# Eight opening transposes written as identity matmuls into fp32 PSUM, in a fused gated mix of a state-space layer and a GELU MLP

## Chip, cores, metric

One core of a Trainium2 chip. The metric is the device time of one execution in microseconds (us). The kernel before takes 213.1 us (median of the six runs that stood beside the result, 212.7 to 213.45).

## The reference, cut to what matters

```python
x = A_x                                            # 1 x 2048 x 640, bf16
g = sigmoid((x * gate_w).sum(-1, keepdims=True))
a = ssm(x, Lambda, B, C, log_dt, Dskip)            # complex diagonal recurrence over 2048 steps
b = gelu(x @ w1 + b1) @ w2 + b2                    # 640 -> 1728 -> 640
return g * a + (1 - g) * b                         # bf16
```

Only the start of `x @ w1` matters here. The kernel multiplies with the 640 features of x on partitions, so x has to be transposed first.

## The kernel before

The first 512 rows of x are wanted as soon as possible. Features 0 to 255 of them are loaded as they lie and transposed by TensorE (eight blocks of 128 x 128); the rest comes through transposing DMAs. Meanwhile TensorE is kept busy by seven matmuls on constants, whose results nobody reads. TensorE's results go into PSUM, in this program eight banks of 512 fp32 columns (`PS[0]` to `PS[7]`), and VectorE copies the transposed blocks from there into `xT`, which the matmuls read. The parts that matter (cuts marked):

```python
load("xna", "sp", ..., xn[0][:, :, 0:256], x2[0:512, 0:256]...)     # 1st transfer of the queue
w1load(0, "sp", 1)            # 2nd: w1 rows 0-127, columns 0-1023 -> tokens ("w1", 0, ...)
w1load(1, "sp", 1.3)          # ... then the other slices
WSPLIT = {1: 6, 3: 6}         # slices that come in two transfers: first 6 column blocks, then 2
...
def f_warm():                                                      # L415
    for n in (512,) * 6 + (256,):
        t = nc.tensor.matmul(PS[4][:, 0:n], one.broadcast_to([128, 128]), one.broadcast_to([128, n]), start=True, stop=True)
    return inc("pe", t)
op("warm", "pe", 2.7, (), [("bank", 4)], f_warm, prio=-1000)

for i, (k, c0, c1) in enumerate(((0, 0, 2), (0, 2, 4), (1, 0, 2), (1, 2, 4))):
    bank = (7, 6, 5, 4)[i]
    pt = PS[bank][:, :].bitcast(BF16)[:, 0:(c1 - c0) * 128]
    def f_xt(k=k, pt=pt, c0=c0, c1=c1):                            # L427: two transposes a bank
        for c in range(c0, c1):
            t = nc.tensor.transpose(pt[:, (c - c0) * 128:(c - c0 + 1) * 128], xn[0][:, c, k * 128:(k + 1) * 128], ident[:, :])
        return inc("pe", t)
    op(f"xt{i}", "pe", ..., ["xna", "ident"], [("bank", bank)], f_xt, prio=-990 + i)
    def f_xc(k=k, pt=pt, c0=c0, c1=c1):                            # L433: VectorE copy PSUM -> SBUF, bf16
        return inc("dve", nc.vector.tensor_copy(out=xT[0][:, k, c0 * 128:c1 * 128], in_=pt))
    op(f"xc{i}", "dve", 0.42, [("bank", bank)], [("xT", 0, k, c0)], f_xc, prio=-2000 + i)
...
# m1_first (L640): x @ w1 for the first 512 rows; the first four matmuls take halves of 256 columns
steps = [(0, 0, 0), (0, 1, 0), (0, 0, 1), (0, 1, 1)] + [(k, jf, None) ...]
```

L640 is the first real work of TensorE; L662 is the rest of `x @ w1`. One line lower in the changed kernel: L641 and L663; the copies are L434 there.

## Time and profile before

| | before |
|---|---|
| span in the profile | 212.1 us |
| TensorE busy | 208.0 us, 98% |
| last of the eight transposes starts | 4.42 us |
| first W1 slice lands | 5.12 us |
| first L640 matmul starts | 5.25 us |
| first L662 matmul starts | 14.34 us |

How to read it: TensorE is nearly always busy, so whatever delays it in the opening delays the end by as much; the lines that show this stand in the prediction. Two instants are worth keeping apart in the opening: when the first weights land, and when TensorE goes from half to full speed. The second can be read without any clock counter from the distance between starts: 256 columns take 213 ns at half speed and 108 at full, 512 columns 427 and 216.

### The profile page before, as it was taken

How to read it: one execution, taken by the hardware profiler on the slowest of the kernel's cores; microseconds unless marked ns; L12 is line 12 of the kernel's file. 1: busy time of each engine (PE TensorE's matmuls, PEld its weight loads, DVE VectorE, ACT ScalarE, POOL GpSimd, SP SyncE). 2: the span in 40 equal slices, each digit the busy share in tenths (PEclk: the TensorE clock that was granted, in tenths of full speed). 3: DMA queues.
4: the chain of work that ended last, by engine and by line, in shares of the span. 5: the costliest groups of instructions: out<-in, count | busy, mean ns of one | idle time of the engine just before them, and what ended most of it. 6: DMA issues, size and time to landing. Idle time of an engine off the chain costs nothing.

```text
span 212.1 us, 2737 instructions
## 1 busy us (share of the span) xinstructions
PE 208.0 (98%) x1088; PEld 104.9 (49%) x1102; DVE 190.1 (90%) x240; ACT 103.0 (49%) x177; POOL 4.2 (2%) x12
## 2 busy tenths in 40 slices
PE   7999999999999999999999999999999999999996
PEld 3444444444564444444464444444446444567775
DVE  2399999999999999999999999899999999499744
ACT  2389556677960353556681063455660027623330
POOL 1000000030000000000000000000010000000000
DMA  5999999999600010075274000004742000005251
GB/s 163 202 279 135 207 171 198 380 222 162 185 12 3 0 49 0 0 85 111 54 59 114 3 0 0 0 2 115 96 96 117 0 3 0 0 0 104 68 140 63
DMA packets 48808, 19.08 MB, mean 90 GB/s; under 512 B 41500, under 2 KB 47772, under 8 KB 48796
## 3 DMA queue, kind: packets, MB, share of 16 engines
q1 hardware_dynamic: 47136, 17.59, 39.7%
q0 software_dynamic: 1600, 1.32, 4.5%
q8 instruction: 8, 0.13, 0.4%
q14 instruction: 4, 0.03, 0.1%
q10 hardware_dynamic: 60, 0.01, 0.0%
HBM read 8.41 MB, written 2.63 MB: 52 GB/s over the span
## 4 chain that ended last, share of the span: by engine, by line
PE 96%; DMA 2%; issue 1%; SPq 0%; DVE 0%
PE ps L662 22%; PE ps L705 20%; PE ps L929 20%; PE ps L978 15%; PE ps L792 7%; PE ps L841 5%; PE ps L640 4%; DMA W1sb<-in_B_w_dram 2%; PE ps L683 1%; PE ps L940 1%; PE ps L806 0%; SPq L333 0%; DVE W1sb L875 0%; PE ps L446 0%
## 5 line engine op out<-in xcount | busy, mean ns | idle before, releaser
L662 PE MATMUL ps<-xT,W1sb 128*128 128x512 bf16 x215 | 47.5, 379 | 0.3
L745 DVE TENSOR_TENSOR_SCAN W<-atab,V 128x1280 bf16<-128x1280 f32 x16 | 44.3, 2812 | 0.3
L705 PE MATMUL ps<-xT,BT 128*128 128x512 bf16 x196 | 43.1, 379 | 0.3 <-issue 0.2
L929 PE MATMUL ps<-Gl,W2sb 128*128 128x512 bf16 (+1 forms) x230 | 42.5, 343 | 0.2
L669 ACT ACTIVATE Gl<-ps,cols 128x512 bf16<-128x512 f32 x44 | 29.9, 694 | 15.5 <-PE ps L662 15.5
L662 PEld LDWEIGHTS ps<-xT,W1sb 128*128 128x128 bf16 x220 | 21.6, 98 | 25.9
L978 PE MATMUL ps<-Hb,CT 128*128 128x512 bf16 x150 | 32.9, 379 | 0.0
L929 PEld LDWEIGHTS ps<-Gl,W2sb 128*128 128x128 bf16 x234 | 22.9, 98 | 19.3
L705 PEld LDWEIGHTS ps<-xT,BT 128*128 128x128 bf16 x200 | 19.5, 98 | 23.7 <-ACT Gt L691 0.4
L714 ACT ACTIVATE U<-ps 128x512 bf16<-128x512 f32 x40 | 23.6, 599 | 14.6 <-PE ps L705 14.5
L947 ACT ACTIVATE E1T<-ps,cols 128x512 bf16<-128x512 f32 (+1 forms) x18 | 9.5, 624 | 36.0 <-PE ps L940 36.0
L978 PEld LDWEIGHTS ps<-Hb,CT 128*128 128x128 bf16 x150 | 14.5, 98 | 17.9 <-DVE V L496 0.6
L986 ACT ACTIVATE E2T<-ps 128x512 bf16<-128x512 f32 x15 | 9.1, 604 | 13.6 <-PE ps L978 13.6
L792 PE MATMUL ps<-W2sb,Gl 128*128 128x320 bf16 x104 | 14.8, 299 | 0.0
L615 DVE SCALAR_TENSOR_TENSOR trf<-xn,gwb 128x640 bf16<-128x640 bf16 x16 | 13.2, 823 | 0.4
L496 DVE TENSOR_TENSOR V<-V,W 128x1280 bf16<-128x1280 bf16 x16 | 12.5, 822 | 0.3
L496 DVE TENSOR_TENSOR Hb<-Hb,V 128x1280 bf16<-128x1280 bf16 x16 | 12.5, 822 | 0.3
L496 DVE TENSOR_TENSOR V<-mr,U 128x2560 bf16<-128x2560 bf16 x8 | 11.9, 1492 | 0.3
L792 PEld LDWEIGHTS ps<-W2sb,Gl 128*128 128x128 bf16 x104 | 10.1, 98 | 4.3 <-issue 0.3
L496 DVE TENSOR_TENSOR Hb<-c,W 128x2560 bf16<-128x2560 bf16 x8 | 11.9, 1491 | 0.2
L496 DVE TENSOR_TENSOR W<-mi,U 128x2560 bf16<-128x2560 bf16 x8 | 11.9, 1484 | 0.0
L496 DVE TENSOR_TENSOR V<-s,W 128x2560 bf16<-128x2560 bf16 x8 | 11.9, 1484 | 0.0
(91 smaller groups left out, 150.8 us busy)
## 6 DMA issues: line engine op xcount, KB each, us to landing
W2sb<-in_B_w_dram SPq DMA_DIRECT2D x1, 2080.0 KB, 8.9
out_dram<-xn SPq DMA_DIRECT2D x3, 640.0 KB, 4.8
xn<-in_A_x_dram POOLq DMA_DIRECT2D x2, 640.0 KB, 7.3
W1sb<-in_B_w_dram SPq DMA_DIRECT2D x3, 256.0 KB, 3.7
trf<-grow SPq DMA_DIRECT2D x3, 256.0 KB, 5.3
xn<-in_A_x_dram SPq DMA_DIRECT2D x1, 640.0 KB, 7.7
W1sb<-in_B_w_dram SPq DMA_DIRECT2D x1, 480.0 KB, 4.6
out_dram<-W1sb SPq DMA_DIRECT2D x3, 160.0 KB, 1.8
```

The costliest lines, as they stand in the source:

```text
L496: return inc("dve", nc.vector.tensor_tensor(out=o, in0=a, in1=b, op=o_))
L615: t = inc("dve", nc.vector.scalar_tensor_tensor(out=scr[:, :], in0=xn[q % 2][:, c, :], scalar=1.0, in1=gwb[:, :], op0=ALU.mult, op1=ALU.mu ...
L662: t = nc.tensor.matmul(PS[bank][:, :], W1sb[:, k, jf * 128:(jf + 1) * 128], xT[q][:, k, :], start=(k == 0), stop=(k == KD - 1))
L669: return inc("act", nc.scalar.activation(Gl[q % 2][:, jf, :], PS[bank][:, :], ACT.Gelu_apprx_tanh, bias=b1col[:, jf:jf + 1]))
L705: t = nc.tensor.matmul(PS[bank][:, :], BT[:, ci, kd, k * 128:(k + 1) * 128], xT[q][:, kd, :], start=(kd == 0), stop=(kd == KD - 1))
L714: return inc("act", nc.scalar.activation(dst, src, ACT.Copy, scale=1.0 if ci == 0 else -1.0))
L745: t = inc("dve", nc.vector.tensor_tensor_scan(out=g[:, ci, :], data0=a, data1=v[:, ci, :], initial=0.0, op0=ALU.mult, op1=ALU.add))
L792: t = nc.tensor.matmul(PS[bank][:, 0:HALF], Gl[q % 2][:, jf, t4 * 128:(t4 + 1) * 128], W2sb[:, jf, cols], start=False, stop=False, skip_gr ...
L841: t = nc.tensor.matmul(PS[bank][:, 0:n], H[b % NHB][:, ci, k, s * 128:(s + 1) * 128], CT[:, ci, k, cols], start=(i == 0), stop=(i == 2 * K ...
L929: t = nc.tensor.matmul(PS[bank][:, 0:t1 - t0], W2sb[:, jf, d * 128:(d + 1) * 128], Gl[q % 2][:, jf, t0:t1], start=(jf == 0), stop=False)
L947: return inc("act", nc.scalar.activation(E1T[:, d, t0:t1], PS[bank][:, 0:t1 - t0], ACT.Identity, bias=cols2[:, 0, d:d + 1]))
L978: t = nc.tensor.matmul(PS[bank][:, :].rearrange("p (s t) -> p s t", s=2), CT[:, ci, k, d * 128:(d + 1) * 128], Hb[:, 2 * (q % 2):2 * (q % ...
```

## The change

The likely intent is that ordinary matmuls should warm the TensorE clock where transposes might not, at the price of copies out of fp32 PSUM. The whole diff:

```diff
-            pt = PS[bank][:, :].bitcast(BF16)[:, 0:(c1 - c0) * 128]
+            pt = PS[bank][:, 0:(c1 - c0) * 128]
...
-                    t = nc.tensor.transpose(pt[:, (c - c0) * 128:(c - c0 + 1) * 128], xn[0][:, c, k * 128:(k + 1) * 128], ident[:, :])
+                    t = nc.tensor.matmul(pt[:, (c - c0) * 128:(c - c0 + 1) * 128], xn[0][:, c, k * 128:(k + 1) * 128], ident[:, :],
+                                         start=(c == c0), stop=(c == c1 - 1), skip_group_check=True)
```

## The prediction

> **What bounds the kernel now.** I read the page first, then the chain of work that ended last in order of time, then the timeline of the first nine microseconds in narrow windows, because the change touches nothing after that. The page's busy line and its chain by engine:
>
> ```profile
> PE 208.0 (98%) x1088; PEld 104.9 (49%) x1102; DVE 190.1 (90%) x240; ACT 103.0 (49%) x177; POOL 4.2 (2%) x12
> ...
> PE 96%; DMA 2%; issue 1%; SPq 0%; DVE 0%
> ```
>
> TensorE is the bound from start to end: 96% of the chain that ended last is its matmuls. What is not TensorE is in the opening microseconds. The chain in order of time begins:
>
> ```profile
> 0.74 0.46 SPq L333
> 1.21 0.06 issue
> 1.26 3.85 DMA W1sb<-in_B_w_dram
> 5.12 0.14 issue
> 5.25 2.94 PE ps L640 x13
> 8.19 0.06 PE ps L446
> ```
>
> Columns: start, length, what. The eight transposes (L427) and their four copies (L433) are not in it. The path starts with the first slice of W1: issued at 1.26, landed 3.85 us later at about 5.12, first real matmul at 5.25. From there the chain is almost unbroken TensorE, so a microsecond won or lost after 5.25 goes through to the end; one before it does not count until the transposes' results come later than the weights.
>
> The timeline shows how far the transposes are from that. One answer for the stretch around them, then one for the matmul that needs them:
>
> ```profile
> 3.69 0.77 PEld L427 LDWEIGHTS ps<-ident,xn 128*128 128x128 bf16 x8 [0.68 <-DMA xn<-in_A_x_dram]
> 3.70 1.04 PE L427 MATMUL ps<-ident,xn 128*128 128x128 bf16 x8
> 4.13 0.93 DVE L433 COPY xT<-ps 128x256 bf16<-128x256 bf16 x4 [2.21 <-PE ps L427]
> ...
> 5.22 2.47 PEld L640 LDWEIGHTS ps<-xT,W1sb 128*128 128x128 bf16 x13 [0.75 <-DVE xT L433]
> 5.25 2.94 PE L640 MATMUL ps<-xT,W1sb 128*128 128x256 bf16 x13 [0.52 <-DMA W1sb<-in_B_w_dram]
> ```
>
> The transposes wait for the x slice, landed at 3.65, and run 3.70 to 4.74. The copies run 4.13 to 5.06; the first one, at most 0.29 long, ends by about 4.43, well before 5.12. TensorE then idles 0.52 us for W1. (The weight load's wait is put down to the copies, but the one that ended last is the DMA that the matmul's own line names.)
>
> Narrow windows give each matmul's start. The seven filling matmuls on constants run from 0.78 to 3.71 and start 427 ns apart at 512 columns; transposes start at 3.78, 3.89, 3.99, 4.10, 4.21, 4.31, 4.42, so 107 ns apart. The first four L640 matmuls, 256 columns wide, start at 5.25, 5.42, 5.63, 5.85 and the next, 512 wide, at 6.06, then 6.30, 6.52, 6.73. So 256 columns cost 213 ns up to 6.06 and 512 columns cost 216 ns from 6.30 on: TensorE ran at half speed until about 6.1 and at full speed after. This is the only thing in the opening that the change could move.
>
> **What the Trainium skill says.** "TensorE: Matmul & The Clock Gate", Part 1 (the HAM clock gate): the array starts at half clock and goes to full after a busy window of about 3.4 us, which is free-running, so the moment differs from run to run. The 427, 107 and 213 ns above are its cold gaps and 216 ns its warm one; the switch at about 6.1 fits. The same page, Part 4 (PE-mode transpose), says of a transpose that the full clock does not engage for it and that "it doesn't count as PE-busy the same way". This is what the change is probably after: as matmuls, the eight would help to warm the clock. The trace neither shows nor refutes it: the clock did rise at 6.1, with 0.85 us of transposes and 0.5 us of idle in the 3.4 us before it.
> "VectorE: DVE Perf Modes", Why PSUM operands drop a tier: a PSUM source gets at most the packed 16-bit double rate, and single rate when fp32. The rows of VectorE agree:
>
> ```profile
> L875 DVE SCALAR_TENSOR_TENSOR W1sb<-ps,gcol,W1sb 128x256 bf16<-128x256 f32 x2 | 1.0, 480 | 0.2 <-PE ps L841 0.2
> L433 DVE COPY xT<-ps 128x256 bf16<-128x256 bf16 x4 | 0.9, 292 | 2.2 <-PE ps L427 2.2
> L875 DVE SCALAR_TENSOR_TENSOR W1sb<-ps,gcol,W1sb 128x128 bf16<-128x128 f32 x1 | 0.4, 352 | 0.1
> L451 DVE CAST cols<-ps 128x29 f32<-128x29 bf16 x1 | 0.2, 190 | 3.2 <-PE ps L446 3.2
> ```
>
> From fp32 PSUM, 128 more columns cost 480 - 352 = 128 ns, 1.00 ns each; from bf16 PSUM, 227 more cost 292 - 190 = 102 ns, 0.45 each. (Different operations, so a slope and no more.)
> "PSUM — Partial Sum Buffer", The four PSUM rules: a matmul that opens a group clears the bank's marks, and a later one without that flag overwrites where the mark is clear. So the second 128 columns of each pair, which do not open a group, land as plain values; a bf16 times an identity summed in fp32 is exact, so the results should be bit-equal.
>
> **The change part by part.** The order of instructions on every engine is the same before and after; I compared them, and only the line numbers differ.
> - TensorE: 8 transposes become 8 matmuls of 128 columns with the same weights (x) and moving operand (identity), bf16 in. Same streaming length, so 107 ns apart at half clock, 8 x 107 = 0.85 us as before, inside 3.70 to 4.74. Change on the path: 0.
> - VectorE: four copies of 256 columns read fp32. Fixed part from the cast: 190 - 29 x 0.45 = 177 ns; with 256 x 1.00 that is about 433 ns against 292, +141 each. They start 213 ns apart today, 79 less than they last; so now about 354 apart. They would end at 4.57, 4.92, 5.27 and 5.63 instead of 4.43 to 5.06.
> - Who needs them: copy 1 the matmul at 5.25 (0.68 to spare, and W1 at 5.12 comes later anyhow); copy 2 the third matmul at 5.63 (0.7 to spare); copies 3 and 4 free the banks that the matmuls at 6.52 and 6.73 write (1.25 and 1.1 to spare), and their data is first read with the second slice at about 7.16 (1.5 to spare). VectorE has nothing else to do until 8.28. Change on the path: 0, with +0.56 us of VectorE work in an idle stretch.
> - The clock: from 5.25 to 6.06 four half-width matmuls took 0.81 us; at full rate they would take 4 x 0.108 = 0.43, and the fifth 0.216 in place of 0.240. The most that an earlier warm-up can give is 0.38 + 0.02 = 0.40 us, 0.19% of 212.8. Whatever it speeds up before 5.12 only waits longer for W1. The later weight slices would allow a 0.40 us lead: the slice for the fifth k lands at 11.78 and is used at about 12.6, the rest of W1 lands at 13.49 and is used at 14.34, so both have over 0.8 to spare.
> Sum: 0 from TensorE and the copies, between 0 and -0.40 from the clock. If the moment of warm-up is set by a free-running window, the matmuls make it earlier only in some executions; I take a quarter of the most, -0.1 us.
>
> **The rivals.**
> 1. The clock warms before 5.25 in nearly every execution. For: the skill's sentence on transposes. Against: the switch at 6.1 came although transposes were part of the window. Time: 212.4.
> 2. The slower copies hold TensorE up. For: the weight load's wait is put down to them, and each gets some 50% longer. Against: 0.68 us to spare. If a copy took 0.8 us instead of 0.43, its chain would delay the third matmul or the banks by a few tenths: 213.2.
> 3. The warm-up shifts the wrong way, or falls by luck later. One further cold window of 3.4 us would cost 1.7 us by the skill's window (an estimate). Nothing favours it; but the three times of before spread over 0.5 us (212.7 to 213.21) with nothing changed, which such luck would explain. Time: up to 214.5.
> 4. VectorE, at 90%, becomes the bound by 0.56 us more. Against: its chain proper starts at 8.28, when the column vectors come from TensorE, and the copies end before it in both kernels. Time: unchanged.
>
> **Range and chances.** The centre is 212.8 - 0.1 = 212.7. The spread of before and rival 1 give the low end, 212.2; rival 2 and luck with the clock the high end, 213.3. Two per cent is 4.3 us, ten times what any term offers: faster 0.01, within 0.98, slower 0.01.
>
> **What would show it.** In the changed kernel: L427 still eight matmuls about 107 ns apart (less if the clock is already up) starting near 3.70; the copies, now a cast from fp32, near 433 ns and not 292; the first L640 matmul still at about 5.25, released by W1; and the start-to-start distance of the first L640 matmuls, 213 or 108 ns for 256 columns, which tells whether the clock came earlier. After 8 us the two traces should differ by one constant shift. The prediction is wrong if the first matmul starts later than 5.3 with a copy named as the cause, if the copies exceed 0.7 us, if the matmuls' cold gap is not 107 ns, or if the shift at the end differs from the shift at 8 us.

## The result, and the profile after

The changed kernel takes 212.96 us (median of 6 runs, 212.84 to 213.53); before 213.1. The ratio is 1.0002, 95% interval 0.9984 to 1.0019: the same. (A ratio is the mean time of one kernel's fast runs over that of the other's of the same rounds, so not quite the ratio of the medians quoted.) The output is correct.

The timeline of the changed kernel around the change (start, length, engine, line, operation; in brackets the idle time before and what ended it):

```profile
3.74 0.48 PEld L427 LDWEIGHTS ps<-ident,xn 128*128 128x128 bf16 x8 [0.72 <-DMA xn<-in_A_x_dram]
3.74 0.66 PE L427 MATMUL ps<-ident,xn 128*128 128x128 bf16 x8
4.10 1.42 DVE L434 CAST xT<-ps 128x256 bf16<-128x256 f32 x4 [2.18 <-PE ps L427]
...
5.08 2.08 PEld L641 LDWEIGHTS ps<-xT,W1sb 128*128 128x128 bf16 x13 [0.86 <-DVE xT L434]
5.11 2.54 PE L641 MATMUL ps<-xT,W1sb 128*128 128x256 bf16 x13 [0.71 <-DMA W1sb<-in_B_w_dram]
```

The four copies stretch from 0.93 to 1.42 us. The eight matmuls took 0.66 us in place of 1.04, and the first thirteen L641 matmuls 2.54 in place of 2.94: this execution ran at full clock early. The chain in order of time agrees; the weights are still what releases the first matmul:

```profile
1.26 3.71 DMA W1sb<-in_B_w_dram
4.98 0.14 issue
5.11 2.54 PE ps L641 x13
```

The group of copies, whose mean the prediction put at 433 ns:

```profile
L434 DVE CAST xT<-ps 128x256 bf16<-128x256 f32 x4 | 1.4, 418 | 2.2 <-PE ps L427 2.2
```

It would be easy to stop here and read "the identity matmuls woke the clock 2.3 us earlier and won 0.5 us". But the starts of the eight in this trace are 80, 77 and then 56 ns apart: the clock rose when only two or three of them had been issued, at about 3.85 us. Up to 3.7 us both kernels had run the same seven filling matmuls. What had not happened yet can't have been the cause. Either this execution met a luckier moment, or the profile before met an unlucky one. That needed more profiles.

### The profile page after: what moved, and what is told of

It reads as the page before. It is cut to its first block, busy times and chain, and to the rows that moved or that the text cites. A ratio compares the mean times of both kernels' runs of the same rounds, so it can differ in the third digit from the quotient of the medians.

```text
span 211.6 us, 2737 instructions
## 1 busy us (share of the span) xinstructions
PE 207.2 (98%) x1088; PEld 104.4 (49%) x1102; DVE 190.6 (90%) x240; ACT 103.1 (49%) x177; POOL 4.2 (2%) x12
## 4 chain that ended last, share of the span: by engine, by line
PE 96%; DMA 2%; issue 1%; SPq 0%; DVE 0%
PE ps L663 22%; PE ps L706 20%; PE ps L930 20%; PE ps L979 15%; PE ps L793 7%; PE ps L842 5%; PE ps L641 4%; DMA W1sb<-in_B_w_dram 2%; PE ps L684 1%; PE ps L941 1%; PE ps L807 0%; SPq L333 0%; DVE W1sb L876 0%; PE ps L447 0%
## 5 line engine op out<-in xcount | busy, mean ns | idle before, releaser
L663 PE MATMUL ps<-xT,W1sb 128*128 128x512 bf16 x215 | 47.5, 379 | 0.3
L663 PEld LDWEIGHTS ps<-xT,W1sb 128*128 128x128 bf16 x220 | 21.6, 98 | 25.9
```

The lines of the kernel that those rows point to most:

```text
L663: t = nc.tensor.matmul(PS[bank][:, :], W1sb[:, k, jf * 128:(jf + 1) * 128], xT[q][:, k, :], start=(k == 0), stop=(k == KD - 1))
```

## The experiments

All twelve gave correct results. Their timed runs also tell how far one kernel's own times spread, which decides here what a difference means.

### 1. Both kernels again, unchanged

> The changed kernel once more, timed in five rounds. My theory: the change leaves the path alone and the clock's moment of warming is luck of the execution, so the ratio to the kernel before is within 0.998 to 1.002, and in this profile full clock may come anywhere from about 3.8 us (as in the changed kernel's first profile) to about 6.1 us (as in the profile of before) or later. Rival: plain matmuls make the clock rise earlier; then full clock comes again by about 3.9 us, and the ratio is about 0.998 (0.4 us of 213) with an interval below 1. Both: the copies 415 to 425 ns, the first L641 matmul 0.14 us after the first W1 slice lands.

> The kernel before, profiled once more. Luck of the window: full clock comes at some other moment than 6.1 us, between about 3.8 and 7 us, and the start of the L640 matmuls' full rate moves with it. Rival, that transposes keep the clock down: full clock not before the first L640 matmuls have run for some 0.8 us, so again at 6 us or later, with the first four L640 matmuls 213 ns apart.

> The kernel before against itself: how far do its own times spread? In the last call it ran from 212.4 to 215.5, three of eleven at 215.0 and more, while the changed kernel stayed within 213.1 to 213.2. If this spread belongs to the kernel before (its clock rising a window later in some executions, some 2 us more), about one in four of these runs is again at 215. If it belonged to that stretch of time, both samples of this call stay within 0.6 us of each other. The profile's full-clock moment comes somewhere from 3.8 to 7 us.

> The changed kernel a third time, for the spread of its times and one more moment of full clock. My theory (same matmul times in both kernels, the clock's moment set by a free-running window): full clock at 3.8 to 4.7 or 6.0 to 6.8 us, whichever the execution meets, as in the four profiles of before and after so far; six times between 212.4 and 213.8, ratio 0.998 to 1.002. Rival (matmuls help the clock): full clock by 4.7 us once more, and a ratio below 0.998.

Measured:

| profile | last of the eight starts | first W1 slice lands | first L640/L641 | full clock from | first L662/L663 | TensorE ends | time of that run |
|---|---|---|---|---|---|---|---|
| before | 4.42 | 5.12 | 5.25 | 6.1 | 14.34 | 210.13 | 213.45 |
| before_again | 4.38 | 5.00 | 5.14 | 4.65 | 13.83 | 209.62 | 212.95 |
| before_again2 | 4.42 | 5.07 | 5.20 | 6.7 | 14.61 | 210.40 | 213.73 |
| after | 4.18 | 4.98 | 5.11 | 3.85 | 13.80 | 209.60 | 212.92 |
| after_again | 4.31 | 5.30 | 5.44 | 4.52 | 14.13 | 209.92 | 213.23 |
| after_again2 | 4.33 | 5.17 | 5.31 | 9.16 | 15.88 | 211.68 | 215.00 |

All in us from the start of the span, but for the last column, which is the device time of the profiled run. (The moment of full clock is recorded in four of the traces; for before and before_again2 it is worked out from the distances of the starts.)

Three things follow. First, from the first L662/L663 matmul to the end of TensorE it is 195.79 us in all six, to 0.01 us: everything that differs lies in the first 16 us. Second, the kernel before also warms early (4.65) and the changed kernel also warms late (9.16), later than the kernel before in any profile. The rival reading is refuted: it had the changed kernel at full clock by 4.7 us every time. Third, where the clock was still cold (before, before_again2, after_again, after_again2) the eight are 106 to 107 ns apart in both kernels, so an identity matmul streams just as a transpose does.

The execution of after_again2 is the most telling one. Its chain:

```profile
1.27 3.91 DMA W1sb<-in_B_w_dram
5.17 0.14 issue
5.31 4.42 PE ps L641 x13
```

The thirteen matmuls that took 2.54 us in a warm execution took 4.42. They start 427 ns apart until 9.1 us. That run took 215.00 us, 1.77 more than the profiled run of after_again, and the first L663 matmul is 1.75 later. The thirteen matmuls alone cost 1.90 us more (4.42 against 2.52 in the chain of after_again), and W1 landed 0.13 earlier: the late clock is all of it.

Times: after_again ratio 0.9974 (0.9922 to 1.0027), its six runs 213.11 to 213.23 while before spread from 212.43 to 215.54; after_again2 ratio 0.9999 (0.9957 to 1.0042), its six runs 212.51 to 215.00. before_again2, which is the kernel before against itself, had 1.0019 (0.9998 to 1.0039). My guess that one in four of the runs of before would be at 215 again did not hold in that call: none was. Over all, 4 of 45 runs of before and 1 of 18 of the changed kernel took over 214 us (one more run of before, at 447.26, is a stray and is left out). Without those, the means are 213.04 for both (41 and 17 runs). The few late runs are too few to say that either kernel has more of them.

A trap in reading: the chain of after_again puts the first L641 matmul down to the copies, where after and after_again2 put it down to W1.

```profile
4.00 0.02 issue
4.02 1.43 DVE xT L434 x4
5.45 2.52 PE ps L641 x13
```

That matmul waits for copy 1 alone, which ended at 4.45. W1 landed at 5.30 and the matmul started at 5.44, 0.135 us after it; in before, after and after_again2 it is also 0.135. The fourth copy happened to end at about the same instant, and the attribution took the later event on the semaphore.

### 2. Do transposes count for the clock?

```diff
-            for n in (512,) * 6 + (256,):
-                t = nc.tensor.matmul(PS[4][:, 0:n], one..., one..., start=True, stop=True)
+            for n in (128,) * 80:                       # warm_tr80
+                t = nc.tensor.transpose(PS[4][:, :].bitcast(BF16)[:, 0:n], one..., ident[:, :])
+            for n in (128,) * 80:                       # warm_mm80, instead
+                t = nc.tensor.matmul(PS[4][:, 0:n], one..., ident[:, :], start=True, stop=True)
```

Both wait for the identity and so start at 1.98 us.

> The kernel before, with its seven filling matmuls replaced by 80 transposes of 128 columns (ones, through the identity). If transposes do not count as activity for the clock, they run 107 ns apart all the way, from about 2.0 to 10.5 us, the clock rises only some 2 to 7 us after the L640 matmuls have begun, and the time is 216 to 221 us. If they count as matmuls do, their distance falls to 56 ns after 2 to 7 us of them, they end between 7 and 10 us, and the L640 matmuls run at full clock from their first, 216 or 108 ns apart. This run has wider spacing only if the clock is down; the results stay right.

> The twin of the run with 80 transposes: 80 plain matmuls of 128 columns with the same operands, same start. Both theories: distance 107 ns at first, 56 ns after 2 to 7 us, done between 7 and 10 us, L640 at full clock from its first matmul. The twin differs from the transposes by over 1 us in the moment of full clock only if transposes do not count.

The timelines, of the run with 80 transposes and then of its twin with 80 matmuls:

```profile
1.98 6.91 PE L415 MATMUL ps<-ident,const-bfloat16-1.0 128*128 128x128 bf16 x80 [1.98 <-DVE ident L406]
8.73 0.61 PE L427 MATMUL ps<-ident,xn 128*128 128x128 bf16 x8
```

```profile
1.98 6.85 PE L415 MATMUL ps<-ident,const-bfloat16-1.0 128*128 128x128 bf16 x80 [1.98 <-DVE ident L406]
8.67 0.61 PE L427 MATMUL ps<-ident,xn 128*128 128x128 bf16 x8
```

6.91 us against 6.85. The single starts are 107 ns apart for the first 44 or so, then one step of 77 (transposes) or 66 (matmuls), then 56 to the end: the clock rose at about 6.7 and 6.6 us. The times are 217.21 and 217.15, because the first L640 matmul has to stand behind the 80, until 9.39 and 9.33. In this pair, one profile each, transposes woke the clock as matmuls did, and they ran at full clock once it was there. The supposed ground of the change is gone: nothing was there to win by the kind of instruction.

### 3. Where is the edge of the copies' room?

```diff
-                return inc("dve", nc.vector.tensor_copy(out=xT[0][...], in_=pt))
+                E.wait("dve", inc("dve", nc.vector.tensor_copy(out=xT[0][...], in_=pt)))
+                return inc("dve", nc.vector.tensor_copy(out=xT[0][...], in_=pt))     # after_copy2
```

> The changed kernel with each of the four copies made twice in a row, the second waiting for the first. My reading of the room: one copy of 0.42 us has room, two do not. Copies about 0.47 us apart from 4.1: second pair done at about 5.9 (needed at 5.3), third at 6.9, fourth at 7.9 (its bank is written by the matmul that now starts at 6.2 to 6.5). So the matmul into the fourth pair's bank starts 1.3 to 1.7 us later than in the changed kernel and the time is 214.3 to 215.0. If the room were larger than I read it, the time stays at 213.

Measured: 214.62 us median (214.15 to 215.47, 4 runs), ratio 1.008 (1.0047 to 1.0114). The time lies in the range; the way there is only half mine. The profile, of a run of 215.08:

```profile
4.92 0.41 DVE L434 CAST xT<-ps 128x256 bf16<-128x256 f32 x1
5.37 0.42 DVE L435 CAST xT<-ps 128x256 bf16<-128x256 f32 x1
5.39 4.42 PE L642 MATMUL ps<-xT,W1sb 128*128 128x256 bf16 x13 [0.67 <-DVE xT L434]
5.84 0.56 PEld L642 LDWEIGHTS ps<-xT,W1sb 128*128 128x128 bf16 x4 [0.35 <-DVE xT L435]
```

The second pair, done at 5.79, held the third matmul from about 5.77 to 5.85, less than 0.1 us. The later pairs held nothing, because in this execution the clock was down until 9.19 us and TensorE itself came late. What made it long is the late clock, as in after_again2. The two runs at 214.15 are about 1.1 us over before; they have no profile, and I take them for executions with an early clock in which the pairs did hold the banks. (An estimate from the traces: the eighth L642 matmul waits for the fourth pair, done here at 7.37; at full clock it would otherwise start 1.08 us after the first, as in after, so at 6.47, and would lose 0.95 us.) So shown is that the room ends between one copy and two at the third matmul; the 1.3 to 1.7 us at the fourth bank is not shown.

### 4. Weights that land earlier

If the copies cost nothing only because W1 comes later, they should show when W1 comes sooner. The first slice in two transfers:

```diff
-        WSPLIT = {1: 6, 3: 6}
+        WSPLIT = {0: 2, 1: 6, 3: 6}                     # before_split, after_split
```

> The kernel before, with the first W1 slice in two transfers (its first two column blocks, 64 KB, then the other six), so that the first weights should land before the present 5.0 to 5.3 us and the transposes' copies come nearer to the path. Expected: the first piece lands at 3.9 to 4.5, the first L640 matmul is then released by copy 1 or by it at 4.4 to 4.6; the rest of the slice lands at 5.1 to 5.5 and holds the fifth matmul. Time the same as before to -0.4 us (ratio 0.998 to 1.000). If the copies were on no path even here, the first matmul follows the landing by 0.14 us.

> The changed kernel with the same two transfers. My theory: the fp32 copies cost nothing in the changed kernel only because W1 lands later; here they show, and the first L641 matmul and the third start 0.1 to 0.3 us later than in the twin with transposes, if the weights have landed by then; at the fifth matmul both wait for the same transfer and the difference is gone. Time equal to the twin's within 0.3 us. Rival (the path never feels the copies): same starts in both.

The first piece landed at 3.90 and 3.88 us. Now copy 1 releases the first matmul: in before_split it ended at 4.40 and the matmul started at 4.455; in after_split it ended at 4.62 and the matmul started at 4.68, 0.055 us after in both. Of the 0.225 us between them, 0.13 is the longer copy (425 against 291 ns) and 0.09 the x slice, which landed later (3.72 against 3.63). So the fp32 copies do cost, once they are on the path, though at this matmul only; the times of the two kernels, 0.14 us apart, do not resolve it. I expected the difference to be gone at the fifth matmul; there it was 5.26 against 5.50, but after_split was at half clock until about 6.2 us and before_split at full clock from 4.19, so this pair does not settle that point.

The times are 213.01 and 213.15 us, ratios 1.0007 (0.9989 to 1.0024) and 1.0016 (0.9999 to 1.0033): the lead bought nothing. The chain of before_split shows where it was given back:

```profile
8.77 3.33 DMA W1sb<-in_B_w_dram
12.10 0.14 issue
12.24 1.89 PE ps L640 x8
```

One more transfer on the issuing queue makes each later one start some 0.5 us later. The last slice (features 512 to 639) was issued at 8.77 in place of 8.23 and landed at 12.10, where the three profiles of before had it at 11.03 to 11.78. The matmul that reads it started 647 ns after the one before in place of 216: 0.43 us lost, more than the lead of 0.31 at the fifth matmul (5.26 against 5.57 in before_again).

So I put the second piece on ScalarE's queue, which is free at that time:

```diff
-                load(f"w1_{k}{i}", eng, ..., prio=prio + 0.1 * i, lat=2.6)
+                late0 = k == 0 and i == 1
+                load(f"w1_{k}{i}", "act" if late0 else eng, ..., prio=-102 if late0 else prio + 0.1 * i, lat=2.6)
```

> The kernel before with the first W1 slice in two transfers, the second of them issued from ScalarE's queue, so that the queue that issues the later slices loses no time. In the run with both on one queue the lead of 0.3 us was given back at 12.1 us, when the last slice landed late. Expected: first L640 matmul at 4.4 to 4.6, the fifth at 5.0 to 5.3, no wait at the last slice, first L662 matmul at 13.4 to 13.6 if the clock is up early; time 0.2 to 0.4 us under before (ratio 0.998 to 0.999). If the lead is lost elsewhere the ratio is 1.000.

> The changed kernel with the same two queues. As the twin with transposes, but with the fp32 copies' 0.12 us at the first matmul and up to 0.25 at the third, hidden again at the fifth by the second transfer: equal to the twin within 0.2 us at the fifth matmul. If the copies were on the path, it would be 0.3 us or more later there.

Both are slower on average, against what I expected, though by less than 2%: 214.75 us (212.98 to 215.4), ratio 1.0067 (1.0022 to 1.0113), and 215.11 (213.15 to 215.2, 5 runs), ratio 1.007 (1.0026 to 1.0114). The timelines, before_split_act and then after_split_act:

```profile
4.49 0.62 PE L428 MATMUL ps<-ident,xn 128*128 128x128 bf16 x8 [0.87 <-DMA xn<-in_A_x_dram]
4.81 0.88 DVE L434 COPY xT<-ps 128x256 bf16<-128x256 bf16 x4 [2.89 <-PE ps L428]
5.16 1.41 PEld L641 LDWEIGHTS ps<-xT,W1sb 128*128 128x128 bf16 x10 [0.22 <-DVE xT L434]
```

```profile
4.39 1.03 PE L428 MATMUL ps<-ident,xn 128*128 128x128 bf16 x8 [0.68 <-DMA xn<-in_A_x_dram]
4.82 1.42 DVE L435 CAST xT<-ps 128x256 bf16<-128x256 f32 x4 [2.90 <-PE ps L428]
5.30 0.13 PEld L642 LDWEIGHTS ps<-xT,W1sb 128*128 128x128 bf16 x2
```

The extra transfer was issued at 0.74 us, together with the x slice, and that landed at 4.34 to 4.44 us, not at 3.65. TensorE idled 0.7 to 0.9 us after its filling matmuls, waiting for x. In the profile of after_split_act full clock came at 9.44 us (a run of 215.11); four of the six runs of before_split_act and four of the five of after_split_act took 214.5 or more: 8 of 11, where the two kernels themselves had 5 of 63 over 214. The profile of before_split_act is of one of the quick runs (212.99), with the clock already up at its eight (56 ns apart), so that its long runs had a late clock is inferred from the twin. Here copy 1 is on the path in both kernels: it started at 4.81 and 4.82, and the first matmul followed at 5.16 and 5.30. That is 0.14 us, the 0.13 by which the copy is longer.

### 5. Less idle time in the opening

Seven matmuls of 128 columns on constants between the eight and the first weights:

```diff
+        def f_fill():
+            for n in (128,) * 7:
+                t = nc.tensor.matmul(PS[0][:, 0:n], one..., one..., start=True, stop=True)
+            return inc("pe", t)
+        op("fill", "pe", 0.4, (), [("bank", 0)], f_fill, prio=-980, after=[xt_last])      # after_fill
```

> The changed kernel with seven more filling matmuls of 128 columns between the eight and the first weights, so that TensorE idles less in the window that decides its clock. If that idle stretch is what can cost a window, full clock never comes after 6.9 us and the times' upper end falls (no time above 213.6), with the median unchanged within 0.2 us[...]. If the clock needed more activity in the usual case too, the median falls by 0.3 us or more.

213.56 us (213.07 to 214.89), ratio 1.0026 (0.9987 to 1.0065): no gain, and three of six runs above the 213.6 that I had set as the limit. In the profile, of the run of 214.89, full clock came at 5.17, and W1 landed already at 4.37 and copy 1 ended at 4.62, but the first L649 matmul had to stand behind the seven until 5.27. And this run's length is no clock matter: TensorE ended at 209.75, but the last output landed 3.8 us later, where it takes 2.0 in the others. So a long run has at least two causes. Each run's span, first to last instruction: 211.6 to 212.6 us in the five runs without a profile (the run of 214.39 has 212.3, so its excess lies outside the span), and 213.7 to 213.8 in the profiled runs with a late clock (after_again2, after_copy2, after_split_act). So none of the six shows such a late clock. With 5 of 63 in the kernels without the filling, none of six proves nothing; whether less idle time keeps the clock from coming late is open.

### What the idle time may have to do with the late clock

An estimate, from the starts in the traces and the window of 3.4 us that the Trainium skill states ("TensorE: Matmul & The Clock Gate", Part 1): in the window that ended with the rise of the clock, TensorE had been streaming for 73% of it (before), 74% (before_again2), 83 to 95% (after, before_again, after_again). In the windows just before a late rise it had been streaming for 71% (after_again2), 71% (after_split_act) and 69% (after_copy2), and the clock stayed down; but before_again2 has one such window at 74%, above the 73% that sufficed in before, so these shares do not part the cases cleanly. If there is an edge, it lies somewhere near 73%, and the opening of both kernels, with 0.8 to 1.1 us of idle TensorE between the fill and the first weights, stands close to it; then a transfer that lands a tenth of a microsecond later could cost a whole window, 1.7 us. The same sum also says that transposes count: without them the passing window of before would have only 49%. This edge is a guess from few windows, not shown: no run varied the idle time alone and with a profile in each case.

No version tried is faster than the two kernels.

## Why the prediction was right

- **TensorE, change on the path 0.** Right: 106 to 107 ns between starts at half clock for transposes and identity matmuls alike, 56 at full clock.
- **The copies, 433 ns each and no cost.** Right: 418 ns, 3% less than the slope gave. They started 331 to 341 ns apart, not 354, and ended at 4.53, 4.86, 5.19 and 5.52, some 0.1 us ahead of the prediction in the last. The first matmul still started 0.135 us after the landing of W1. That the rooms of 0.7 us are real but not large is shown by doubling the copies (third matmul held) and by the earlier weights (first matmul later by the 0.13 us of the longer copy).
- **The clock, between 0 and -0.40 us, a quarter taken.** The size was right: the warm first thirteen matmuls save 0.40 us (2.54 against 2.94) over an execution that warms at 6.1. The -0.1 as an effect of the change is not shown and I now think it is zero: transposes warm the clock as matmuls do (6.7 against 6.6 us with 80 of each), and both kernels warm early or late by the execution. It is far below what the intervals resolve, so the total was not hurt. That the two medians stand 0.14 us apart, close to the -0.1, is luck: the ratio of the same runs, 1.0002, points the other way.
- **Rival 1** (warm before 5.25 in nearly every execution) falls with after_again2. **Rival 2** (copies hold TensorE) needs doubled copies or earlier weights. **Rival 4** (VectorE) did not occur: 195.79 us of TensorE after the opening in both.
- **Rival 3** was under-rated. "Nothing favours it", I wrote of a window lost; it happens, in the changed kernel's 215.00 us, where the late clock cost the first thirteen matmuls 1.9 us (the prediction's estimate for one whole window was 1.7, its time up to 214.5). It happens to both kernels, so it belongs in the spread and not in the difference.
- The test "the two traces should differ by one constant shift after 8 us" holds: 0.54 us at the first L662/L663 matmul (14.34 to 13.80) and 0.54 at the end of TensorE (210.13 to 209.60). Of it, 0.14 is W1's landing and 0.40 the clock, neither of them the change's.
- One of the signs of being wrong, a first matmul later than 5.3 "with a copy named as the cause", did appear to the letter in after_again: 5.44, with the copies in the chain. It was a bad sign, not a wrong prediction: the view named copy 4, while W1 landed at 5.30, after copy 1 (4.45), and the matmul followed W1 by the usual 0.135 us. A sign should ask which wait ended last, not which one a view names.

## What to carry to other kernels

When two profiles differ by a few tenths, first profile the old kernel again: here its own two further profiles span 0.8 us, more than the change's whole possible effect. Order in time refutes causes cheaply: a clock that rose when two of the eight changed instructions had been issued was not raised by them. Work that ended 0.69 us before the transfer that everybody waited for (4.43 against 5.12) could get 43% slower for nothing (418 against 292 ns), but an additional transfer to bring that one forward had its own price, at the queue (0.5 us later starts) or beside it (the x slice, at 4.34 to 4.44 in place of 3.63 to 3.72).

## What the Trainium skill lacked or had wrong

- "TensorE: Matmul & The Clock Gate", Part 4 (PE-mode transpose), says that the full clock does not engage for transposes and that they don't count as PE-busy in the same way. Here 80 bf16 transposes raised the clock after 4.7 us, at 6.7 us, 80 identity matmuls of the same size at 6.6; from then on the transposes ran 56 ns apart. In before_split, whose trace records the rise at 4.19, the last step between transposes is 56 ns too.
- The same page, Part 1, gives the time to full clock as a busy window of about 3.4 us and tells authors to avoid idle gaps of over some 3.4 us. It does not say how busy a window must be. In these runs two short gaps, together about 1.0 us (0.1 and 0.9 in after_again2), went with a clock that came at 9.16 us in place of 4 to 7 and cost 1.9 us; the edge near 73% busy is a guess.
- The same page, Part 1, has the moment of full clock vary by some 500 ns from run to run and the penalty below 1% of a typical span. Here the changed kernel's three profiles had it at 3.85, 4.52 and 9.16 us, 5.3 us apart. Two of these executions took 212.92 and 215.00 us, 1.0% apart: 1.88 of the 2.08 us is the clock, 0.20 the landing of W1. So an effect below 1% can't be read from a few runs.
- No page has it that the end can vary too: in after_fill the last output landed 3.8 us after the last matmul, in the other profiles 2.0.
